# A fused attention and mixer kernel: the opening dealt anew, the x of 20 units transposed by DMA, and the last group split into two PSUM banks

## The chip, the cores and the metric

The kernel runs on one core of a Trainium2 chip. The metric is the device time of one execution in microseconds. Before the change, the median of three runs is 374.11 us (373.75 to 374.95).

## What is computed

```python
def _attn_ref(q, k, v):                       # (8, 12, 448, 64) each
    scores = scale * q @ k.transpose(0, 1, 3, 2) - np.log(S)
    return sigmoid(scores) @ v                # no row sum: every score stands alone

x = attn.transpose(0, 2, 1, 3).reshape(8, 448, 768)
h = np.maximum(x^T @ w_tok1, 0) @ w_tok2      # mixes the 448 tokens, 256 wide
u = x + h^T
h2 = np.maximum(u @ w_ch1, 0) @ w_ch2         # mixes the 768 channels, 1536 wide
out = u + h2                                  # (8, 448, 768), float32
```

Inputs are float32. The kernel converts them to fp16 while they are loaded, and accumulates in float32.

## The kernel before

**Units and cycles.** The 12 heads of a batch are dealt into three *units* of four heads (`NU = 3`), and the kernel goes through 24 units in 24 *cycles* c = 3b + u. For one unit, `qk` (L137) makes the scores, in seven steps j of 64 keys: four 64x64 matmuls into one two-bank PSUM tile (tag "qk", two of them), then one ACT sigmoid of 128x896 into `att`. `av` (L162) multiplies `att` with v into two PSUM banks and DVE casts them to `xT`, x with channels on the partitions. x is then turned so that tokens are on the partitions (`xn`), in one of two ways: `xtrans` (L197) with eight PE transposes and a DVE copy, or `xtrans_dma` (L191) with one DMA transpose issued by SP. `tok1` (L213) and `ytrans` (L240) are the token mixer; `ytrans` ends with a DVE addition into `ut`, which is u with channels on the partitions.

**The channel mixer** of a batch, `stage2` (L434), needs `ut` of all three units. `ch1` makes 12 blocks of 6 matmuls (448 columns each), `ch2` six groups of 12 matmuls (384 columns), `ch2_last` (L338) the last 64 tokens in 24 matmuls that use half the array each; DVE adds u and SP issues the output's DMAs. For batches 1 to 7, u comes from `un`, a DMA transpose of `ut` (`utrans`, L262); batch 0 has no `un`, and PE adds u with further matmuls against the identity.

**How they are woven.** The loop at L537 emits, for each cycle, the scores of that cycle's unit and the rest of the work of the unit before, and cuts `stage2` of an earlier batch into small pieces that `work(share)` pours in at three places of every cycle. `starts` (L535) says in which cycle a batch's pieces begin, and the pieces are spread evenly over the shares until the next start. `ON_DMA` (L534) says which units' x is turned by DMA. For those, `tok1` and `ytrans` come one cycle later than for units turned by PE (`mixed`, L541). A batch's `utrans` comes with its last unit's `ytrans`.

**k and q.** They must be transposed before `qk`. Batches 0 and 1 do this on PE (`pe_transpose`, L123: 14 transposes and a DVE copy, tag "m"). From batch 2 on, DVE regroups them (`relayout`, six copies, L97, recorded at L103) and SP issues two DMA transposes (`dma_transpose`, recorded at L116: `tr_k`, then `tr_q`) at the end of the cycle with u = 1 of the batch before. All use one queue of SP, which issues in program order and also carries `xtrans_dma`, `utrans` and the outputs.

**Loads.** All inputs are loaded by POOL's queue, in program order (from L381), with at most eight of them outstanding. After the opening's loads, a copy to `gate` (L602) holds back the loads of the next batches until `tr_q` of the batch in between has landed.

**The opening.** Units 0 to 2 are woven by hand (the table `between`, L476), then the *fourth cycle* (L513 to L532): the scores of unit 0 of batch 1 woven with the chain av, xtrans, tok1, ytrans of batch 0's unit 2, and the first two blocks of ch1. `keep_warm` (L449) issues matmuls on a constant while PE would wait for the first loads. PSUM tiles other than the scores' share four banks (tag "m").

Of the kernel before, what the change touches and what calls it, by code (L numbers as in the profile page):

```python
# [10 lines left out]
FP32 = mybir.dt.float32  # L11
# [9 lines left out]
NJ = 7  # L21
# [5 lines left out]
def kernel(  # L27
# [59 lines left out]
    def load(b, t, src, u0, u1):  # L87

        for g in range(2):
            dst = raw_tile(b, t)[64 * g : 64 * g + 64, u0:u1, :, :, :]  # L90
            heads = src[b, 6 * g + 2 * u0 : 6 * g + 2 * u1]
            nc.gpsimd.dma_start(  # L92
                out=dst.rearrange("p u hi j e -> p (u hi) (j e)"),
                in_=heads.rearrange("h (p j) e -> p h (j e)", j=NJ),
            )
# [27 lines left out]
    def pe_transpose(b, t, u, j0=0, j1=NJ):  # L123
        if j0 == 0:
            tps[t] = pp.tile([128, NJ, 128], FP16, tag="m", bufs=4, name=f"tp_{t}_{b}_{u}")
        ps = tps[t]
        for j in range(j0, j1):
            for hi in range(2):
                nc.tensor.transpose(  # L129
                    out=ps[64 * hi : 64 * hi + 64, j, :],  # L130
                    in_=raw[b, t][:, u, hi, j, :],
                    identity=ident[:, :],
                )
        nc.vector.tensor_copy(out=tr_tile(b, t)[:, u, j0:j1, :], in_=ps[:, j0:j1, :])
# [62 lines left out]
    def xtrans(b, u):  # L197
        ps = pp.tile([128, 4, 2, 128], FP16, tag="m", bufs=4, name=f"xb_{b}_{u}")
        for g in range(2):
            for t in range(4):  # L200
                nc.tensor.transpose(  # L201
                    out=ps[:, t, g, :],
                    in_=xTs[b % 2][:, u, g, 128 * t : 128 * t + 128],
                    identity=ident[:, :],
                )
        nc.vector.tensor_copy(
            out=xn_tile(b)[:, u, :, :, :].rearrange("s g t d -> s t g d"),
            in_=ps[:, :, :, :],
        )
# [27 lines left out]
            else:  # L237
                nc.scalar.activation(out=dst, in_=src, func=RELU)  # L238

    def ytrans(b, u, in_qk_slot=False):  # L240
        if in_qk_slot:
            both = pp.tile([128, 2, 512], FP32, tag="qk", bufs=2, name=f"yt_{b}_{u}")
        for g in range(2):
            db = NU * g + u
            if in_qk_slot:
                ps = both[:, g, :]
            else:
                ps = pp.tile([128, 512], FP32, tag="m", bufs=4, name=f"yt_{b}_{db}")
            for tcb in range(2):
                nc.tensor.matmul(  # L250
                    out=ps[:, 0:S],
                    lhsT=h1[b][:, tcb, g, u, :],
                    rhs=w2[:, tcb, :, :],
                    start=(tcb == 0),
                    stop=(tcb == 1),
                )
            nc.vector.tensor_tensor(  # L257
                out=uts[b % 2][:, db, 0:S], in0=xTs[b % 2][:, u, g, 0:S], in1=ps[:, 0:S], op=ADD
            )
# [76 lines left out]
                )  # L336

    def ch2_last(b, n0=0, n1=NCB):  # L338
        if n0 == 0:
            acc[b] = pp.tile([128, 512], FP32, tag="m", bufs=4, name=f"c2_{b}_3")  # L340
        ps = acc[b]
        for n in range(n0, n1):
            for g in range(2):
                nc.tensor.matmul(  # L344
                    out=ps[64 * g : 64 * g + 64, 0:DH],
                    lhsT=h2[b][:, n, 384:448],
                    rhs=c2[:, n, DH * g : DH * g + DH],
                    start=(n == 0),
                    stop=(n == NCB - 1 and b in un),
                )  # L350
        if n1 < NCB:
            return
        o = pa.tile([128, DH], FP32, tag="outl", bufs=2, name=f"o_{b}_3")
        if b in un:
            for g in range(2):
                part = slice(64 * g, 64 * g + 64)
                nc.vector.tensor_tensor(
                    out=o[part, :].rearrange("s (u d) -> s u d", d=128),
                    in0=un[b][0:64, NU * g : NU * g + NU, 3, :],
                    in1=ps[part, 0:DH].rearrange("s (u d) -> s u d", d=128),  # L360
                    op=ADD,
                )
        else:
            for n in range(NU):
                for g in range(2):
                    nc.tensor.matmul(
                        out=ps[64 * g : 64 * g + 64, 128 * n : 128 * n + 128],
                        lhsT=uts[b % 2][:, NU * g + n, 384:448],
                        rhs=ident[:, :],
                        start=False,  # L370
                        stop=(n == NU - 1),
                    )
            nc.vector.tensor_copy(out=o[:, :], in_=ps[:, 0:DH])
        for g in range(2):
            nc.sync.dma_start(
                out=orow[b, NJ - 1][:, DH * g : DH * g + DH],
                in_=o[64 * g : 64 * g + 64, :],
            )


# [8 lines left out]
    nc.vector.memset(w1[64:128, 3, :], 0.0)  # L389
    load(0, "q", q, 1, 2)  # L390
    load(0, "k", k, 1, 2)
    load(0, "v", v, 0, 1)
    tok_rows = moe_w_tok1.rearrange("(p j) t -> j p t", j=NJ)
    for par in range(2):
# [3 lines left out]
            in_=tok_rows[0:6].rearrange("(t par) p c -> par p t c", par=2)[par],  # L398
        )
    nc.gpsimd.dma_start(out=w1[0:64, 3, :], in_=tok_rows[NJ - 1])  # L400
    load(0, "q", q, 2, NU)
    load(0, "k", k, 2, NU)
    nc.gpsimd.dma_start(
        out=w2s[:, :, :], in_=moe_w_tok2.rearrange("(tc t) s -> t tc s", tc=2)
    )
# [4 lines left out]
    def load_c1(half):  # L410
        cols = slice(CC // 2 * half, CC // 2 * half + CC // 2)
        nc.gpsimd.dma_start(
            out=c1[:, :, cols],
            in_=moe_w_ch1.rearrange("(db d) c -> d db c", db=NDB)[:, :, cols],
        )
# [2 lines left out]
    load(1, "q", q, 1, 2)  # L418
    load(1, "k", k, 1, 2)
    load(1, "v", v, 0, 1)  # L420
    load_c1(1)
    load(1, "q", q, 2, NU)
    load(1, "k", k, 2, NU)
    load(1, "v", v, 1, NU)
    load(2, "k", k, 0, NU)
    load(2, "q", q, 0, NU)
    for half in range(2):
        part = slice(NCB // 2 * half, NCB // 2 * half + NCB // 2)
        nc.gpsimd.dma_start(
            out=c2[:, part, :],  # L430
            in_=moe_w_ch2.rearrange("(cb c) d -> c cb d", cb=NCB)[:, part, :],
        )
# [11 lines left out]

    N_CYCLES = NU * B
    N_FIRST = 4
    heat = pp.tile([128, 512], FP32, tag="m", bufs=4, name="heat")

    def keep_warm(n):  # L449
        for _ in range(n):  # L450
            nc.tensor.matmul(
                out=heat[:, 0:256], lhsT=warm[:, 0:128], rhs=warm[:, :], start=True, stop=True
            )

    keep_warm(19)
    pe_transpose(0, "q", 0)
    keep_warm(3)
    pe_transpose(0, "k", 0, 0, 2)
    pe_transpose(0, "k", 0, 2, NJ)

    def regroup_w2():
# [4 lines left out]
    def tp(b, u, t, j0=0, j1=NJ):  # L466
        return lambda: pe_transpose(b, t, u, j0, j1)
# [4 lines left out]
    def tok(u, *tcbs):  # L472
        return lambda: tok1(0, u, True, tcbs)
# [2 lines left out]
    between = [  # L476
        [
            [],
            [],
            [tp(0, 1, "q", 0, 4)],  # L480
            [tp(0, 1, "q", 4, NJ)],
            [tp(0, 1, "k", 0, 4)],
            [tp(0, 1, "k", 4, NJ)],
            [],
        ],
        [
            [value(0, 0, 3)],
            [value(0, 3, NJ)],
            [tp(0, 2, "q")],
            [lambda: xtrans(0, 0)],  # L490
            [tp(0, 2, "k"), regroup_w2],
            [tok(0, 0)],
            [tok(0, 1)],
        ],
        [
            [value(1, 0, 3)],
            [lambda: ytrans(0, 0)],
            [value(1, 3, NJ)],
            [tp(1, 0, "q")],
            [lambda: xtrans(0, 1)],  # L500
            [tp(1, 0, "k")],
            [tok(1, 0, 1)],
        ],
    ]
    for u, steps in enumerate(between):
# [4 lines left out]

    qk(1, 0, 0)  # L513
    av(0, 2, 0, 5)
    ytrans(0, 1)
    qk(1, 0, 1)
    av(0, 2, 5, NJ)
    pe_transpose(1, "q", 1)
    qk(1, 0, 2)
    xtrans(0, 2)  # L520
    ch1(0, 0, 0, 4)
    qk(1, 0, 3)
    tok1(0, 2, relu_on_vector=True)
    pe_transpose(1, "k", 1)
    ch1(0, 1, 0, 4)
    qk(1, 0, 4)
    ytrans(0, 2, in_qk_slot=True)
    qk(1, 0, 5)
    for d in (4, 5):
        for cb in range(2):  # L530
            ch1(0, cb, d, d + 1)
    qk(1, 0, 6)  # L532

    ON_DMA = range(2 * NU, N_CYCLES - 2)  # L534
    starts = [N_FIRST, N_FIRST + NU] + [NU * b + 5 for b in range(2, B - 1)] + [N_CYCLES + 1]  # L535
    pending, copies = [], []
    for c in range(N_FIRST, N_CYCLES + 1):  # L537
        b, u = divmod(c, NU)
        here = c < N_CYCLES
        before = divmod(c - 1, NU)  # L540
        mixed = [n for n in (c - 2, c - 1) if (n == c - 1) != (n in ON_DMA)]  # L541
        if c in starts:
            n = starts.index(c)
            first, slots = c, 3 * max(starts[n + 1] - c, NU)
# [35 lines left out]
        if here:  # L580
            qk(b, u, 3)
            qk(b, u, 4)
        work(2)
        for n in mixed:
            tok1(*divmod(n, NU))
        if here:
            qk(b, u, 5)
            qk(b, u, 6)
        if c == N_FIRST:
            copies = pieces  # L590
        work(3)
        for n in mixed:
            ytrans(*divmod(n, NU))
# [49 lines left out]
```

## Time and profile before

| | |
|---|---|
| median of the runs | 374.11 us |
| the profiled execution | 374.46 us, its span 372.7 us |
| mean granted TensorE clock | 0.995 |
| PE busy | 359.8 us |
| ch1 (L282), 576 matmuls | 115.8 us busy |
| ch2 (L305), 576 matmuls | 100.3 us busy |
| ACT, 168 sigmoids of 128x896 (L152) | 158.7 us busy |
| SP's queue q1 / POOL's queue q0 | 28.98 MB / 21.70 MB |
| last PE instruction ends / span ends | 368.2 us / 372.7 us |

The page gives the busy time of each engine and the groups of instructions that make it up; PE's busy time includes the latency of matmuls that overlap, so durations of a step are read below from the starts of consecutive steps. The timeline gives single steps with the idle time before them and what ended it; the stage view gives busy times, granted clock, DMA share and throughput for a stretch; the DMA view gives what each queue moved in a stretch and how long an issue took to land.

### The profile page before, as it was taken

What the parts mean: (1) busy time and instruction counts of PE and PEld (TensorE: products, weight loads), DVE (VectorE), ACT (ScalarE), POOL (GpSimd) and SP (SyncE); (2) the same over time, 40 slices, a digit from 0 to 9 for tenths busy, and PEclk for the clock granted to TensorE, in tenths of its full rate; (3) what the DMA queues carried; (4) which work ended last, traced back from release to release, by engine and by line L of the source; (5) the groups of instructions that cost most, each with busy time, mean ns of one, the idle gap of its engine ahead of it and who ended that gap; (6) DMA issues with size and microseconds to landing.
All of it is one profiled execution on the core that took longest, in us unless ns stands there. A gap on an engine that the chain in (4) does not pass through costs nothing.

```text
span 372.7 us, 7520 instructions
## 1 busy us (share of the span) xinstructions
PE 359.8 (97%) x3254; PEld 196.8 (53%) x3254; DVE 184.7 (50%) x328; ACT 171.6 (46%) x211; POOL 50.4 (14%) x87
## 2 busy tenths in 40 slices
PE   6999999999999999999999999999999999999995
PEld 4554456564545554555445555555445555565562
DVE  2466566327643655375453554465453353734532
ACT  2995544546566445455455544455444555000000
POOL 8844300500030003100040001200000000000000
PEclk9899999999999999999999999999999999999999
DMA  7999999799998697994999389974960451036014
GB/s 100 168 201 206 204 210 193 142 220 219 180 167 127 114 165 130 143 209 98 192 147 185 72 169 159 179 141 103 195 101 16 98 123 28 0 81 153 2 42 106
DMA packets 99840, 51.14 MB, mean 137 GB/s; under 512 B 73504, under 2 KB 96736, under 8 KB 99808
## 3 DMA queue, kind: packets, MB, share of 16 engines
q1 hardware_dynamic: 76384, 28.98, 42.0%
q0 software_dynamic: 23424, 21.70, 38.1%
q8 instruction: 25, 0.41, 0.4%
q14 instruction: 7, 0.06, 0.0%
HBM read 43.38 MB, written 11.01 MB: 146 GB/s over the span
## 4 chain that ended last, share of the span: by engine, by line
PE 87%; DMA 7%; ACT 2%; DVE 1%; SPq 1%; issue 1%; POOL 1%; DVEq 0%; POOLq 0%
PE c L282 26%; PE c L305 26%; PE qk L145 10%; PE xa L172 9%; DMA tr_q<-rel_q 6%; PE tk L224 5%; PE c L344 4%; PE yt L250 4%; ACT att L152 2%; PE xb L201 1%; DMA raw_k<-in_k_dram 1%; PE tp_k L129 1%; SPq L116 1%; PE tp_q L129 0%; POOL raw_q L92 0%
## 5 line engine op out<-in xcount | busy, mean ns | idle before, releaser
L152 ACT ACTIVATE att<-qk,att_bias 128x896 f16<-128x896 f32 x168 | 158.7, 1008 | 103.5 <-PE qk L145 103.5
L282 PE MATMUL c<-ut,c 128*128 128x448 f16 x576 | 115.8, 353 | 0.0
L305 PE MATMUL c<-c,h 128*128 128x384 f16 x576 | 100.3, 327 | 0.0
L290 DVE TENSOR_SCALAR h<-c 128x448 f16<-128x448 f32 x96 | 59.7, 624 | 58.7 <-PE c L282 58.6
L282 PEld LDWEIGHTS <-c 128*128 128x128 f16 x576 | 53.2, 98 | 58.3 <-issue 12.8
L305 PEld LDWEIGHTS <-h 128*128 128x128 f16 x576 | 54.0, 98 | 42.9 <-issue 9.3
L145 PE MATMUL qk<-tr_q,tr_k 64*64 64x448 f16 x672 | 53.5, 365 | 4.5 <-DMA tr_q<-rel_q 2.3
L315 DVE TENSOR_TENSOR o<-un,c 128x384 f32<-128x384 f16 x42 | 23.3, 554 | 56.6 <-PE c L305 56.0
L181 DVE CAST xT<-xa 128x448 f16<-128x448 f32 x48 | 27.7, 619 | 22.2 <-PE xa L172 22.2
L238 ACT ACTIVATE h<-tk 128x256 f16<-128x256 f32 x42 | 13.8, 381 | 52.5 <-PE tk L224 52.5
L172 PE MATMUL xa<-att,raw_v 64*64 64x448 f16 x672 | 37.6, 352 | 0.0
L257 DVE TENSOR_TENSOR ut<-xT,yt 128x448 f16<-128x448 f16 x48 | 27.6, 616 | 9.9 <-PE yt L250 9.7
L145 PEld LDWEIGHTS <-tr_k 64*64 64x64 f16 x672 | 15.6, 105 | 28.4 <-issue 25.2
L172 PEld LDWEIGHTS <-raw_v 64*64 64x64 f16 x672 | 23.5, 107 | 9.2 <-issue 0.8
L224 PE MATMUL tk<-xn,w 128*128 128x256 f16 x192 | 24.9, 273 | 0.7 <-DVE h L234 0.7
L602 POOL COPY gate<-tr_q 128x2 f16<-128x2 f16 x5 | 0.9, 184 | 164.8 <-DMA tr_q<-rel_q 164.8
L250 PE MATMUL yt<-w,h 128*128 128x448 f16 x96 | 22.2, 354 | 0.7 <-DVE ut L257 0.7
L224 PEld LDWEIGHTS <-w 128*128 128x128 f16 x192 | 18.5, 98 | 6.1 <-issue 1.2
L344 PE MATMUL c<-c,h 128*64 128x384 f16 x192 | 17.1, 328 | 0.0
L92 POOL DMA_DIRECT2D raw_k<-in_k_dram x24 | 15.2, 643 | 9.7 <-DMA c<-in_moe_w_ch_dram 4.7
L92 POOL DMA_DIRECT2D raw_q<-in_q_dram x24 | 15.5, 664 | 6.0 <-DMA c<-in_moe_w_ch_dram 4.7
L250 PEld LDWEIGHTS <-h 128*128 128x128 f16 x96 | 8.6, 98 | 10.2 <-issue 2.7
(41 smaller groups left out, 116.2 us busy)
## 6 DMA issues: line engine op xcount, KB each, us to landing
out_dram<-o SPq DMA_DIRECT2D x48, 192.0 KB, 2.7
c<-in_moe_w_ch_dram POOLq DMA_DIRECT2D x4, 1152.0 KB, 14.5
raw_k<-in_k_dram POOLq DMA_DIRECT2D x12, 336.0 KB, 5.5
raw_q<-in_q_dram POOLq DMA_DIRECT2D x12, 336.0 KB, 9.0
raw_v<-in_v_dram POOLq DMA_DIRECT2D x12, 336.0 KB, 12.1
out_dram<-o SPq DMA_DIRECT2D x16, 96.0 KB, 2.1
raw_q<-in_q_dram POOLq DMA_DIRECT2D x12, 112.0 KB, 6.6
raw_k<-in_k_dram POOLq DMA_DIRECT2D x12, 112.0 KB, 5.7
```

Source lines behind the costliest of these rows:

```text
L92: nc.gpsimd.dma_start(out=dst.rearrange("p u hi j e -> p (u hi) (j e)"), in_=heads.rearrange("h (p j) e -> p h (j e)", j=NJ),)
L145: nc.tensor.matmul(out=ps[64 * g : 64 * g + 64, hi, 0:S], lhsT=tr[b, "k"][64 * hi : 64 * hi + 64, u, j, 64 * g : 64 * g + 64], rhs=tr[b, " ...
L152: nc.scalar.activation(out=att[b, u][:, :, j, :], in_=ps[:, :, 0:S], func=SIGMOID, bias=bias_t[:, :], scale=att_scale,)
L172: nc.tensor.matmul(out=ps[g][64 * hi : 64 * hi + 64, 0:S], lhsT=raw[b, "v"][64 * g : 64 * g + 64, u, hi, j, :], rhs=att[b, u][64 * g : 64 ...
L181: nc.vector.tensor_copy(out=xTs[b % 2][:, u, g, 0:S], in_=ps[g][:, 0:S])
L224: nc.tensor.matmul(out=ps[:, tcb, :, :], lhsT=w1[:, t, cols], rhs=xn[b][:, u, :, t, :], start=(t == 0), stop=(t == 3),)
L250: nc.tensor.matmul(out=ps[:, 0:S], lhsT=h1[b][:, tcb, g, u, :], rhs=w2[:, tcb, :, :], start=(tcb == 0), stop=(tcb == 1),)
L257: nc.vector.tensor_tensor(out=uts[b % 2][:, db, 0:S], in0=xTs[b % 2][:, u, g, 0:S], in1=ps[:, 0:S], op=ADD)
L282: nc.tensor.matmul(out=ps[:, 0:S], lhsT=c1[:, BY_UNIT[d], 128 * cb : 128 * cb + 128], rhs=uts[b % 2][:, BY_UNIT[d], 0:S], start=(d == 0), ...
L290: nc.vector.tensor_scalar(out=h2[b][:, cb, :], in0=ps[:, 0:S], scalar1=0.0, scalar2=None, op0=MAX)
L305: nc.tensor.matmul(out=ps[:, 0:DH], lhsT=h2[b][:, cb, 128 * t : 128 * t + 128], rhs=c2[:, cb, cols], start=(cb == 0), stop=(cb == NCB - 1 ...
L344: nc.tensor.matmul(out=ps[64 * g : 64 * g + 64, 0:DH], lhsT=h2[b][:, n, 384:448], rhs=c2[:, n, DH * g : DH * g + DH], start=(n == 0), stop ...
```

## The change

It has five parts.

1. **Loads.** q and k of batch 0's unit 2 go ahead of v of unit 0 and the token weights. q, k of batch 1's unit 2 and k, q of batch 2 go ahead of the second half of c1 (the first weights of the channel mixer).
2. **Warm matmuls.** 21, 5 and 3 instead of 19 and 3 ahead of the first scores, and 6 + 3 new ones within unit 0's cycle.
3. **The opening's order.** q and k of unit 1 are transposed later in unit 0's cycle, in whole tiles; q of unit 2 also there; batch 0's first `ytrans` moves up into unit 1's cycle; the second stands at the head of the fourth cycle, where ch1's pieces move behind unit 2's tok1 and k's transposes ahead of it. `ytrans` of unit 2 uses the "m" banks.
4. **The loop.** `ON_DMA` grows from units 6 to 21 to units 4 to 23. Batch 0's channel work is spread over the four cycles 4 to 7 (before: 4 to 6), batch 1's over three, 8 to 10 (before: 7 to 10). Units 22 and 23 are mixed in the cycle after the last scores. In cycle 4 the relayouts are handed out a share earlier.
5. **The last group.** `ch2_last` of batch 7 adds u on PE with six matmuls against the identity, uses one bank per half, and evacuates one half on DVE and the other on ACT, whose own queue then issues that half's output.

```diff
     def ch2_last(b, n0=0, n1=NCB):
+        final = b == B - 1
         if n0 == 0:
-            acc[b] = pp.tile([128, 512], FP32, tag="m", bufs=4, name=f"c2_{b}_3")
-        ps = acc[b]
+            acc[b] = [
+                pp.tile([128, 512], FP32, tag="m", bufs=4, name=f"c2_{b}_3_{g}")
+                for g in range(2 if final else 1)
+            ]
+        parts = [slice(0, 64), slice(64, 128)]
+        ps = [acc[b][g if final else 0][parts[g], 0:DH] for g in range(2)]
+        add_on_pe = final or b not in un
...
+        for n in range(NU if add_on_pe else 0):
+            for g in range(2):
+                nc.tensor.matmul(
+                    out=ps[g][:, 128 * n : 128 * n + 128],
+                    lhsT=uts[b % 2][:, NU * g + n, 384:448],
+                    rhs=ident[:, :],
...
+        for g in range(2):
+            if final and g == 1:
+                nc.scalar.activation(out=o[parts[g], :], in_=ps[g], func=COPYF)
+            elif add_on_pe:
+                nc.vector.tensor_copy(out=o[parts[g], :], in_=ps[g])
...
+            queue = nc.scalar if final and g == 1 else nc.sync
+            queue.dma_start(
+                out=orow[b, NJ - 1][:, DH * g : DH * g + DH], in_=o[parts[g], :]
             )
...
     load(0, "q", q, 1, 2)
     load(0, "k", k, 1, 2)
+    load(0, "q", q, 2, NU)
+    load(0, "k", k, 2, NU)
     load(0, "v", v, 0, 1)
...
     load(1, "v", v, 0, 1)
-    load_c1(1)
     load(1, "q", q, 2, NU)
     load(1, "k", k, 2, NU)
-    load(1, "v", v, 1, NU)
     load(2, "k", k, 0, NU)
     load(2, "q", q, 0, NU)
+    load_c1(1)
+    load(1, "v", v, 1, NU)
...
-    keep_warm(19)
+    new_heat()
+    keep_warm(21)
     pe_transpose(0, "q", 0)
+    keep_warm(5)
+    pe_transpose(0, "k", 0, 0, 2)
     keep_warm(3)
-    pe_transpose(0, "k", 0, 0, 2)
     pe_transpose(0, "k", 0, 2, NJ)
...
     between = [
         [
             [],
-            [],
-            [tp(0, 1, "q", 0, 4)],
-            [tp(0, 1, "q", 4, NJ)],
-            [tp(0, 1, "k", 0, 4)],
-            [tp(0, 1, "k", 4, NJ)],
+            [new_heat, lambda: keep_warm(6)],
+            [lambda: keep_warm(3)],
+            [tp(0, 1, "q")],
+            [tp(0, 1, "k")],
+            [tp(0, 2, "q")],
             [],
         ],
         [
             [value(0, 0, 3)],
             [value(0, 3, NJ)],
-            [tp(0, 2, "q")],
+            [tp(0, 2, "k")],
             [lambda: xtrans(0, 0)],
-            [tp(0, 2, "k"), regroup_w2],
-            [tok(0, 0)],
+            [tok(0, 0), regroup_w2],
             [tok(0, 1)],
+            [lambda: ytrans(0, 0)],
         ],
         [
             [value(1, 0, 3)],
-            [lambda: ytrans(0, 0)],
             [value(1, 3, NJ)],
             [tp(1, 0, "q")],
             [lambda: xtrans(0, 1)],
+            [tok(1, 0)],
+            [tok(1, 1)],
             [tp(1, 0, "k")],
-            [tok(1, 0, 1)],
         ],
     ]
...
+    ytrans(0, 1)
     qk(1, 0, 0)
-    av(0, 2, 0, 5)
-    ytrans(0, 1)
+    av(0, 2, 0, 6)
     qk(1, 0, 1)
-    av(0, 2, 5, NJ)
+    av(0, 2, 6, NJ)
     pe_transpose(1, "q", 1)
     qk(1, 0, 2)
     xtrans(0, 2)
-    ch1(0, 0, 0, 4)
+    pe_transpose(1, "k", 1)
     qk(1, 0, 3)
     tok1(0, 2, relu_on_vector=True)
-    pe_transpose(1, "k", 1)
-    ch1(0, 1, 0, 4)
     qk(1, 0, 4)
-    ytrans(0, 2, in_qk_slot=True)
+    for cb in range(2):
+        ch1(0, cb, 0, 4)
+    ytrans(0, 2)
     qk(1, 0, 5)
-    for d in (4, 5):
-        for cb in range(2):
-            ch1(0, cb, d, d + 1)
+    for cb in range(2):
+        ch1(0, cb, 4, 5)
     qk(1, 0, 6)
-
-    ON_DMA = range(2 * NU, N_CYCLES - 2)
-    starts = [N_FIRST, N_FIRST + NU] + [NU * b + 5 for b in range(2, B - 1)] + [N_CYCLES + 1]
+    for cb in range(2):
+        ch1(0, cb, 5, 6)
+
+    ON_DMA = range(N_FIRST, N_CYCLES)
+    starts = [N_FIRST] + [NU * b + 5 for b in range(1, B - 1)] + [N_CYCLES + 1]
...
-        mixed = [n for n in (c - 2, c - 1) if (n == c - 1) != (n in ON_DMA)]
+        mixed = [n for n in (c - 2, c - 1) if (n == c - 1) != (n in ON_DMA) or not here]
...
+        if c == N_FIRST:
+            copies = pieces
         work(2)
...
-        if c == N_FIRST:
-            copies = pieces
         work(3)
```

More of the change, by code (lines that the diff above doesn't have):

```diff
@@ L238, in tok1, with ytrans @@
                 nc.scalar.activation(out=dst, in_=src, func=RELU)
-    def ytrans(b, u, in_qk_slot=False):
-        if in_qk_slot:
-            both = pp.tile([128, 2, 512], FP32, tag="qk", bufs=2, name=f"yt_{b}_{u}")
+    def ytrans(b, u):
         for g in range(2):
             db = NU * g + u
[L245 to L248, printed above, removed]
+            ps = pp.tile([128, 512], FP32, tag="m", bufs=4, name=f"yt_{b}_{db}")
             for tcb in range(2):
@@ L344, in ch2_last @@
                 nc.tensor.matmul(
-                    out=ps[64 * g : 64 * g + 64, 0:DH],
+                    out=ps[g],
                     lhsT=h2[b][:, n, 384:448],
@@ L348, in ch2_last @@
                     start=(n == 0),
-                    stop=(n == NCB - 1 and b in un),
+                    stop=(n == NCB - 1 and not add_on_pe),
                 )
@@ L352, in ch2_last @@
             return
-        o = pa.tile([128, DH], FP32, tag="outl", bufs=2, name=f"o_{b}_3")
-        if b in un:
-            for g in range(2):
-                part = slice(64 * g, 64 * g + 64)
+        for n in range(NU if add_on_pe else 0):
[4 more added lines that the diff above has]
+                    rhs=ident[:, :],
+                    start=False,
+                    stop=(n == NU - 1),
+                )
+        o = pa.tile([128, DH], FP32, tag="outl", bufs=2, name=f"o_{b}_3")
+        for g in range(2):
[3 more added lines that the diff above has]
+                nc.vector.tensor_copy(out=o[parts[g], :], in_=ps[g])
+            else:
                 nc.vector.tensor_tensor(
-                    out=o[part, :].rearrange("s (u d) -> s u d", d=128),
+                    out=o[parts[g], :].rearrange("s (u d) -> s u d", d=128),
                     in0=un[b][0:64, NU * g : NU * g + NU, 3, :],
-                    in1=ps[part, 0:DH].rearrange("s (u d) -> s u d", d=128),
+                    in1=ps[g].rearrange("s (u d) -> s u d", d=128),
                     op=ADD,
                 )
[L363 to L377, printed above, removed]
+            queue = nc.scalar if final and g == 1 else nc.sync
+            queue.dma_start(
+                out=orow[b, NJ - 1][:, DH * g : DH * g + DH], in_=o[parts[g], :]
             )
@@ L400 @@
     nc.gpsimd.dma_start(out=w1[0:64, 3, :], in_=tok_rows[NJ - 1])
-    load(0, "q", q, 2, NU)
-    load(0, "k", k, 2, NU)
     nc.gpsimd.dma_start(
@@ L446 @@
     N_FIRST = 4
-    heat = pp.tile([128, 512], FP32, tag="m", bufs=4, name="heat")
+    heat = {}
     def keep_warm(n):
@@ L451, in keep_warm, with new_heat @@
             nc.tensor.matmul(
-                out=heat[:, 0:256], lhsT=warm[:, 0:128], rhs=warm[:, :], start=True, stop=True
-            )
-    keep_warm(19)
+                out=heat[0][:, 0:256],
+                lhsT=warm[:, 0:128],
+                rhs=warm[:, :],
+                start=True,
+                stop=True,
+            )
+    def new_heat():
+        heat[0] = pp.tile([128, 512], FP32, tag="m", bufs=4, name="heat")
+    new_heat()
+    keep_warm(21)
     pe_transpose(0, "q", 0)
+    keep_warm(5)
+    pe_transpose(0, "k", 0, 0, 2)
     keep_warm(3)
-    pe_transpose(0, "k", 0, 0, 2)
     pe_transpose(0, "k", 0, 2, NJ)
```

## The prediction

> **What bounds the kernel now.** I read the page's totals first, then the PE's waits, then the stages, then the DMA queue behind the one wait that is left.
>
> ```profile
> PE 359.8 (97%) x3254; PEld 196.8 (53%) x3254; DVE 184.7 (50%) x328; ACT 171.6 (46%) x211; POOL 50.4 (14%) x87
> ```
>
> PE is the bound: whatever leaves its stream is gained in full, and whatever makes it wait is lost in full. The view of PE's waits holds one repeated wait on a DMA, at the first scores of a batch:
>
> ```profile
> PE qk L145 <- DMA tr_q<-rel_q: 2.3, 4, 0.7
> ```
>
> Four times, 0.7 us at most: k and q transposed by SP's DMA arrive just in time in the steady batches. Batch 2's pair (tr_k, tr_q), used first at cycle 6, is not among the four: it landed at 66.9 (issue 61.66 plus 5.2), PE came at 69.22. Cycle 6 is where I look hardest, since the change brings PE there earlier. SP's part and the DMA by stage, from the timeline and the stage view (last two columns: mean busy share, GB/s):
>
> ```profile
> 56.75 4.87 SPq L116 DMA_TRANSPOSE tr_k<-rel_k  x1
> 61.66 3.30 SPq L116 DMA_TRANSPOSE tr_q<-rel_q  x1
> ```
>
> ```profile
> 56.00:58.00 2.00, 2.00 (x33) 1.33 (x25) 2.00 (x5) 2.00 (x3) 0.00 (x0) 1.00 1.16 210
> 58.00:60.00 2.00, 2.00 (x13) 1.03 (x11) 2.00 (x5) 0.43 (x1) 0.00 (x0) 1.00 1.89 153
> 60.00:62.00 2.00, 2.00 (x23) 1.13 (x22) 1.55 (x3) 0.89 (x1) 0.00 (x0) 1.00 0.61 127
> 62.00:64.00 2.00, 2.00 (x17) 1.29 (x15) 0.49 (x1) 1.01 (x2) 0.00 (x0) 1.00 1.24 266
> ```
>
> Until 58 the engines are full (1.16) with POOL's loads, the last being c2; the transposes really run from 61 to 66.3. How the queues share shows in a later xn transpose (issued at 190.8) beside loads; first 191 to 194.5, then 195 to 200:
>
> ```profile
> q0 software_dynamic: 811, 0.70, 126.1%
> ...
> xn<-xT SPq DMA_TRANSPOSE x1, 12.0
> ```
>
> ```profile
> q0 software_dynamic: 862, 0.74, 90.6%
> q1 hardware_dynamic: 862, 0.22, 32.9%
> ```
>
> For 3.7 us SP's queue (q1) moves nothing; then it gets one packet for one of the loads, 256 B against 896 B. So 256 KB took 12.0 us; the same transpose alone took 3.1 (issue 185.65).
>
> **The opening, until 40.5 (nothing, and it is swallowed).** ACT sets it:
>
> ```profile
> 8.27 12.86 ACT L152 ACTIVATE att<-qk,att_bias 128x896 f16<-128x896 f32 x14 [5.88 <-PE qk L145]
> 21.55 6.52 ACT L152 ACTIVATE att<-qk,att_bias 128x896 f16<-128x896 f32 x7 [0.42 <-PE qk L145]
> ```
>
> 21 activations at 0.92 with one gap of 0.42. The added warm matmuls lie in waits: 2 more of 0.11 us before q lands (wait 0.47), 2 more before k (0.34), 3 beside the copy that k's second half awaits (0.38), 9 in a cycle that ACT paces; uncovered they cost 0.11 each. They aim at the clock (third last column):
>
> ```profile
> 7.80:11.20 3.40, 2.12 (x38) 1.23 (x34) 1.14 (x3) 2.93 (x4) 3.40 (x7) 1.00 1.11 150
> 11.20:14.70 3.50, 3.43 (x38) 1.67 (x41) 0.92 (x3) 3.46 (x4) 3.46 (x7) 0.51 1.18 162
> ```
>
> Half clock for 3.4 us, but inside the ACT run without a gap: curing it gains nothing. The Trainium skill, "TensorE: Matmul & The Clock Gate" (HAM oscillation), asks for a PE-idle gap over about 3.4 us before the clock falls; here it fell after a stretch with 2.12 us busy of 3.40 and no wait over 0.92, so the row decides. By the rule the warm matmuls would do nothing, by the row they may keep the clock: zero in the sum either way.
>
> q and k of unit 2 pass v of unit 0 on POOL's queue: two places of 224 KB at some 150 GB/s, 3.0 us. v landed near 11.1 to 11.7 and is read at 14.18, so it comes about when it is needed (0 to 1 us late).
>
> Walking units 1 and 2 by the rows (qk 0.31 with what follows, 14 transposes 0.51, xb 0.54, tok half 0.5, yt 0.86; DVE: cast 0.58, xn 0.69, tr copy 0.61, relu 0.42): tok now directly follows xtrans and waits for xn, so unit 2's first activation comes 0.7 later and unit 3's near 30.1 instead of 28.3, with one ytrans (0.86) more done. In the fourth cycle these waits go or shrink:
>
> ```profile
> 37.28 0.54 PE L250 MATMUL yt<-w,h 128*128 128x448 f16 x2 [0.71 <-DVE ut L257]
> 40.50 0.38 PE L145 MATMUL qk<-tr_q,tr_k 64*64 64x448 f16 x4 [0.87 <-ACT att L152]
> ```
>
> New ones come: xtrans for the cast (0.6), tok for xn (0.5). By the walk cycle 4's av starts near 40.5, before 40.68: 0.2 gained, between 1.5 gained and 1 lost.
>
> **Cycles 4 and 5.** Batch 0's work is spread over 12 shares, not 9: per share 12 matmuls of 0.19 instead of 15. Cycle 4 took 14.86 (40.68 to 55.54); less 12 matmuls, 12.6. Cycle 5, 55.54 to 69.22: unit 4's xtrans (0.54), tok (0.97) and ytrans (0.85) leave, work falls from 8.57 to 6.6: 9.35 from av to the scores of cycle 6. PE arrives at 40.5 + 12.6 + 9.35 = **62.4**.
>
> Half of c1 now lands behind 1,792 KB more: at 205 GB/s 9 us later, near 46.5 (before 23.20 + 14.4); block 6 is multiplied near 50, so it costs nothing with 3 us to spare. Batch 2's k, q land before 41 and wait for nobody. The relayouts start a share earlier, the last of k ends 12 us after av: tr_k is issued near **52.4**, 4.3 us sooner.
>
> But all loads together are as many bytes in a full queue, so c2 still ends at 58 to 61. tr_k at 52.4 stands in front of that queue: first packet some 3.7 us later, then one 256 B packet per 1,536 B packet of c2, a few hundred of its 2,688 before c2 is out. What remains, nearly 1.3 MB, takes the 5.3 us that it took before. A little is won (tr_q no longer waits for SP's issue): I take tr_q at **66.3**. Bounds: 61.6 if nothing hindered it (52.4 plus the 9.2 from 92.01 to 101.2); 64.4 if no DMA time were lost (c2 out at 58.5, 5.3 for the pair, 0.6 until the landing shows); 68 if mixing delays c2's last packets. The Trainium skill, "DMA: Bandwidth & Descriptors" (Queues, rings and completion order), says that an engine round-robins between queues per packet; the alternation agrees, the 3.7 us of nothing does not. By the rule alone tr_k would get some 400 packets more before c2 ends: 0.4 us less in the sum.
>
> So the wait moves from cycle 4 to cycle 6, 3.9 us, and a faster or slower opening only changes its length.
>
> **From cycle 6 on,** measured from its scores (69.22 before), PE does more: 24 matmuls of batch 0's second layer at 0.163 = 3.91, two additions 0.32, unit 4's tok and ytrans 1.82: +6.05. It does less: xtrans of units 5, 22 and 23, start to next start 0.54 + 0.54 + 0.45 = 1.53, as in
>
> ```profile
> 60.13 0.61 PE L201 MATMUL xb<-ident,xT 128*128 128x128 f16 x8
> ```
>
> xn by DMA there: unit 5's beside loads, up to 12.8 us after about 70, needed at 85; unit 23's with 7 us of work ahead of it: hidden. If they weren't, tok waits for the rest. Cycle 8 now has the steady shape (un ahead of tr_k on SP), so cycle 9 may get the steady wait of 0.6: +0.5.
>
> **The tail.**
>
> ```profile
> 368.21 1.13 DVE L357 TENSOR_TENSOR o<-un,c 64x384 f32<-64x384 f16 x2 [1.52 <-PE c L344]
> 368.78 1.11 SPq L375 DMA_DIRECT2D out_dram<-o  x2
> ```
>
> Six more matmuls cost 0.26 (82.88 to 83.14 in batch 0's last group); the second DVE half (0.57) goes beside the first, on ACT: between the relu's 0.38 for 256 columns and the sigmoid's 1.01 for 896, estimated 0.51. Its DMA goes from ACT, which no row shows; SP's issues took 0.47 to 0.64. Gain 0.3, between 0.6 and -0.6. Batch 0's last group has two copies instead of one, beside PE: nothing.
>
> **Sum.** (66.3 - 69.22) + 6.05 - 1.53 + 0.5 - 0.3 = **+1.8 us**. On the profiled execution, 374.46 (span 372.7, the 1.76 around it taken as unchanged), that is 376.3; the median of the runs, 374.11, lies 0.35 lower, so I predict **375.9 us**.
>
> **Rivals.**
> - *Not slower, but faster: the transposes come in time.* If SP's queue gets through beside c2, tr_q lands at 61.6 to 62.4 and PE does not wait: (62.4 - 69.22) + 4.7 = -2.1, 372.0 us. For it: the issue is 4.3 us earlier, out DMAs did get through beside loads. Against: the 12.0 us row. It decides from a landing before 63.4. Chance 0.14.
> - *Shared without loss:* tr_q at 64.4: -0.1, 374.0 us. For it: the engines are full either way; against: 58 to 62 moved only 127 to 153 GB/s while both ran. 0.28.
> - *Forecast,* 375.9 us: 0.44.
> - *Worse mixing:* c2 itself reaches PE late (its second half is read near 62), tr_q at 68: +3.5, 377.6 us. 0.14.
>
> Range 372.6 to 377.6: it leaves out some of the first and last. Faster by over 0.3% (about what a measurement can tell from no change) 0.14, within 0.28, slower 0.58.
>
> **What would show it.** Right: PE's waits list qk <- DMA tr_q once with 3 to 5 us, ending near 66; tr_k issued near 52 with a landing over 9 us; cycle 4's av at 39.5 to 41; no PE xb for units 4, 5, 22, 23; clock 1.00 from 11.2 to 14.7. Wrong: no such wait, or c2 ending before 57; or an opening that loses several us (v late at 14, ACT gaps), since past 66 it counts in full.

## The result and the profile after

The changed kernel takes 379.58 us (median of 5 runs, 379.25 to 380.56), the kernel before 374.01 us on the same chip (5 runs, 373.75 to 374.95). The ratio is 1.0153, with a 95% interval of 1.0131 to 1.0175: slower by 5.6 us, where +1.8 was forecast. The profiled span grew from 372.7 to 378.7 us, the mean granted clock fell from 0.995 to 0.991.

The page's totals of the changed kernel:

```profile
PE 361.4 (95%) x3244; PEld 197.8 (52%) x3244; DVE 181.9 (48%) x322; ACT 172.3 (45%) x212; POOL 50.9 (13%) x87
```

PE executes 10 matmuls fewer than before and is busy 1.6 us longer, and its share fell from 97% to 95%. So part of the loss is matmuls that run slower, part is waiting. PE's waits (us in total, times, longest):

```profile
PE qk L145 <- DMA tr_q<-rel_q: 7.2, 6, 4.0
PE c L300 <- DMA c<-in_moe_w_ch_dram: 1.5, 1, 1.5
```

Before, tr_q was waited for 2.3 us in all and c2 not at all. The wait of 4.0 us is the one forecast for cycle 6; the other five are the steady ones, 0.6 us each on average. SP's part of the timeline shows what brings it:

```profile
52.09 10.43 SPq L116 DMA_TRANSPOSE tr_k<-rel_k  x1
62.56 3.74 SPq L116 DMA_TRANSPOSE tr_q<-rel_q  x1
```

SP reaches tr_k 4.66 us earlier than before (56.75), but its issue instruction holds SP for 10.43 us instead of 4.87. SP can therefore issue tr_q only at 62.56, later than before (61.66). tr_k landed 13.0 us after its issue, tr_q 5.1. The DMA view gives what the queues moved from 56 to 60 (packets, MB, share of 16 engines; q0 is POOL's queue, q1 SP's):

```profile
q0 software_dynamic: 450, 0.68, 93.7%
q1 hardware_dynamic: 479, 0.12, 22.5%
```

One packet for one, 256 B of tr_k against 1.5 KB of c2, as forecast. In the 3.6 us after the issue (52 to 55.7) q1 does not appear at all; its first packet moves at 56.0. PE's timeline then shows both waits and what follows them:

```profile
63.17 0.65 PE L300 MATMUL c<-c,h 128*128 128x384 f16 x3 [1.49 <-DMA c<-in_moe_w_ch_dram]
67.82 0.96 PE L145 MATMUL qk<-tr_q,tr_k 64*64 64x448 f16 x8 [4.00 <-DMA tr_q<-rel_q]
68.54 2.86 PE L172 MATMUL xa<-att,raw_v 64*64 64x448 f16 x28
```

The last line matters most: the same 28 matmuls of av take 1.52 us in cycle 4 (start 39.88) and 1.49 in cycle 7 (82.46). The stage view explains it (length; busy time of PE, PEld, DVE, ACT, POOL; then granted clock, DMA share, GB/s):

```profile
64.00:66.00 2.00, 0.00 (x0) 0.00 (x0) 0.00 (x0) 0.00 (x0) 0.00 (x0) 0.93 1.28 269
66.00:70.00 4.00, 2.18 (x24) 1.28 (x28) 0.00 (x0) 1.48 (x2) 1.96 (x4) 0.50 0.76 134
70.00:72.50 2.50, 2.50 (x23) 1.08 (x16) 1.07 (x2) 1.10 (x2) 2.50 (x5) 0.50 1.10 167
```

PE stands still from 64 to 66; by the trace's records the clock is at half from 65.72, 1.9 us into the wait, to 72.55. In the opening it is the other way round:

```profile
11.20:14.70 3.50, 2.98 (x65) 1.95 (x65) 1.87 (x3) 3.50 (x5) 3.50 (x6) 1.00 1.23 181
```

The half clock that the kernel before shows there (0.51) is gone. The tail is as described:

```profile
374.37 0.33 PE L356 MATMUL c<-ident,ut 128*64 128x128 f16 x6
374.74 0.55 DVE L368 COPY o<-c 64x384 f32<-64x384 f32 x1 [1.68 <-PE c L356]
374.77 0.48 ACT L366 ACTIVATE o<-c 64x384 f32<-64x384 f32 x1 [40.49 <-PE c L356]
375.29 0.55 ACTq L377 DMA_DIRECT2D out_dram<-o  x1
```

DVE and ACT evacuate side by side. From PE's last instruction (374.7) to the end of the span it is 4.0 us now, 4.5 before.

**Theory** at this point: the loss is one place, cycle 6, with two parts. tr_k, issued into the load queue, delays c2 and holds SP, so tr_q lands 1.5 us later than forecast; and the wait of 4.0 us drops PE's clock for what follows. **Rivals:** the loss is spread (unit 4 and 5's work moved past cycle 6, more steady waits); or it comes from the new load order or the opening.

### The profile page after: what moved, and what is told of

Read it like the earlier page. It is cut to its first block, busy times and chain, and to the rows that moved or that the text cites. A ratio compares the mean times of both kernels' runs of the same rounds, so it can differ in the third digit from the quotient of the medians.

```text
span 378.7 us, 7505 instructions
## 1 busy us (share of the span) xinstructions
PE 361.4 (95%) x3244; PEld 197.8 (52%) x3244; DVE 181.9 (48%) x322; ACT 172.3 (45%) x212; POOL 50.9 (13%) x87
## 4 chain that ended last, share of the span: by engine, by line
PE 83%; DMA 10%; ACT 2%; DVE 2%; SPq 2%; issue 1%; POOL 0%; POOLq 0%
PE c L300 25%; PE c L277 25%; PE qk L145 10%; PE xa L172 9%; DMA tr_q<-rel_q 9%; PE tk L224 5%; PE c L345 4%; PE yt L245 4%; ACT att L152 2%; SPq L116 2%; DMA raw_k<-in_k_dram 1%; DVE xT L181 1%; PE tp_k L129 1%; DVE xn L206 0%; POOL raw_q L92 0%
## 5 line engine op out<-in xcount | busy, mean ns | idle before, releaser
L300 PEld LDWEIGHTS <-h 128*128 128x128 f16 x576 | 54.2, 98 | 44.9 <-issue 11.0
L172 PE MATMUL xa<-att,raw_v 64*64 64x448 f16 x672 | 38.5, 359 | 0.0
L172 PEld LDWEIGHTS <-raw_v 64*64 64x64 f16 x672 | 24.4, 109 | 9.1 <-issue 1.7
L366 ACT ACTIVATE o<-c 64x384 f32<-64x384 f32 x1 | 0.5, 485 | 40.5 <-PE c L356 40.5
```

The costliest lines, as they stand in the source:

```text
L172: nc.tensor.matmul(out=ps[g][64 * hi : 64 * hi + 64, 0:S], lhsT=raw[b, "v"][64 * g : 64 * g + 64, u, hi, j, :], rhs=att[b, u][64 * g : 64 ...
L300: nc.tensor.matmul(out=ps[:, 0:DH], lhsT=h2[b][:, cb, 128 * t : 128 * t + 128], rhs=c2[:, cb, cols], start=(cb == 0), stop=(cb == NCB - 1 ...
```

## The experiments

Every ratio is against the kernel before on the same chip, with its 95% interval.

**1. Matmuls on a constant ahead of the wait.**

```diff
+        if c == 2 * NU:
+            new_heat()
+            keep_warm(36)
```

> The changed kernel with 36 warm matmuls (3.9 us at full clock) ahead of cycle 6's first scores, where PE waited 4.0 us for tr_q. Theory (the wait is set by the DMA, and the half clock from 65.7 to 72.6 behind it is a second cost of its own): the data still lands near 67.8, the clock stays at 1.00, and the 4.7 us of PE work that ran at half clock take 2.4 us less: about 377.2 us. Rival (the half clock costs nothing, since something else holds PE there): 379.6 us as the changed kernel. If warm matmuls themselves delay the scores: 380 us or more.

Measured: 376.39 us, 1.005 [1.003, 1.007]. PE's timeline of this kernel at cycle 6:

```profile
64.01 4.09 PE L452 MATMUL heat<-warm 128*128 128x256 f16 x36
68.11 0.57 PE L145 MATMUL qk<-tr_q,tr_k 64*64 64x448 f16 x8
68.48 1.52 PE L172 MATMUL xa<-att,raw_v 64*64 64x448 f16 x28
```

The transposes are no earlier (tr_k 52.04 and 10.71 long, tr_q 62.79), PE goes on no earlier, but the clock stays at 1.00 and av takes 1.52 instead of 2.86. From the first scores to cycle 7's av it is 12.38 us (68.11 to 80.49), in the changed kernel 14.64 (67.82 to 82.46): 2.3 us that only the clock costs. The profiled spans differ by more, 3.1 us (375.6 against 378.7): the five steady waits are shorter too, 2.1 us in all instead of 3.2, for no reason that I could find. The medians differ by 3.2 us, the ratios by some 3.9, since the kernel before was 0.5 us slower on this chip.

**2. The second half of c2 is not loaded.** Blocks 6 to 11 multiply the first half's rows instead: as many matmuls on other numbers, so that only the time is read.

```diff
-    for half in range(2):
+    for half in range(1):
...
-                rhs=c2[:, cb, cols],
+                rhs=c2[:, cb % 6, cols],
...
-                    rhs=c2[:, n, DH * g : DH * g + DH],
+                    rhs=c2[:, n % 6, DH * g : DH * g + DH],
```

> The changed kernel without the load of c2's second half (1,152 KB); blocks 6 to 11 of the second layer multiply the first half's rows instead, so this part of the computation is changed and only the time is read. Theory (tr_k and tr_q are held up by the loads queued ahead of them): loads end near 57 instead of 62.8, SP's issue of tr_k falls from 10.4 to 4 to 6 us, tr_q lands near 61 to 63, the wait at cycle 6 is at most 1 us, the wait for c2 is gone, the clock does not fall: 372 to 373 us. Rival (the transposes are slow by themselves, or the loop's new shape costs the time elsewhere): 378 to 379.6 us.

Measured: 372.37 us, 0.9935 [0.9912, 0.9958]. SP's timeline, and below it PE's, of this kernel:

```profile
52.04 4.80 SPq L116 DMA_TRANSPOSE tr_k<-rel_k  x1
56.88 3.32 SPq L116 DMA_TRANSPOSE tr_q<-rel_q  x1
```

```profile
62.33 0.57 PE L145 MATMUL qk<-tr_q,tr_k 64*64 64x448 f16 x8 [0.20 <-DMA tr_q<-rel_q]
62.70 1.52 PE L172 MATMUL xa<-att,raw_v 64*64 64x448 f16 x28
```

The issue is at the same time, but takes 4.80 instead of 10.43, and tr_q lands when PE arrives. The whole loss is gone: it is c2 that stands between the early issue and an early landing. This run also tests the rest of the forecast's sum, as a whole and not term by term: with PE at 62.33 its terms give (62.33 - 69.22) + 4.72 = -2.2 us, and the profiled spans differ by -1.9 (370.8 against 372.7).

**3. Units 4 and 5 back on PE, batch 0 spread as before;** the rest of the change stays.

```diff
-    ON_DMA = range(N_FIRST, N_CYCLES)
-    starts = [N_FIRST] + [NU * b + 5 for b in range(1, B - 1)] + [N_CYCLES + 1]
+    ON_DMA = range(2 * NU, N_CYCLES)
+    starts = [N_FIRST, N_FIRST + NU] + [NU * b + 5 for b in range(2, B - 1)] + [N_CYCLES + 1]
```

> The changed kernel with units 4 and 5 turned by PE again and batch 0's work spread over three cycles as before; opening, loads, units 22 and 23, and the last group stay as changed. Theory (only the earlier arrival at cycle 6 costs): PE comes to cycle 6 near 68.4, about when tr_q lands, no clock fall; the gains of the rest remain, 0.8 (opening) + 1.0 (two xtrans) + 0.2 (last group): about 372 us. Rival (the opening, the load order or the last group costs): 375 us or more.

Measured: 374.17 us, 0.9979 [0.9959, 0.9999]. The loss is gone, since PE now has work until about 70, but less is gained than expected. tr_k, issued even earlier (50.49), still takes 10.79 us of SP, c2 is still waited for (1.4 us), and av of cycle 6 starts at 70.23, later than before (69.62), although cycle 4's av (39.77) was 0.9 earlier. The opening's gain is handed back at c2.

**4. The loop's part alone,** put on the kernel before.

```diff
-    ON_DMA = range(2 * NU, N_CYCLES - 2)
-    starts = [N_FIRST, N_FIRST + NU] + [NU * b + 5 for b in range(2, B - 1)] + [N_CYCLES + 1]
+    ON_DMA = range(N_FIRST, N_CYCLES)
+    starts = [N_FIRST] + [NU * b + 5 for b in range(1, B - 1)] + [N_CYCLES + 1]
...
-        mixed = [n for n in (c - 2, c - 1) if (n == c - 1) != (n in ON_DMA)]
+        mixed = [n for n in (c - 2, c - 1) if (n == c - 1) != (n in ON_DMA) or not here]
...
+        if c == N_FIRST:
+            copies = pieces
         work(2)
...
-        if c == N_FIRST:
-            copies = pieces
         work(3)
```

> The kernel before with the loop's change alone (units 4 to 23 by DMA, batch 0 over four cycles, relayouts a share earlier); its opening, load order and last group as before. Theory: the loop alone makes the loss: PE comes to cycle 6 some 0.8 us later than in the changed kernel and waits 3 to 4.5 us, the clock falls: 379.5 to 380.5 us. Rival (the new load order or opening is needed for the loss): 372 to 375 us.

Measured: 376.72 us (374.97 to 378.68), 1.006 [1.0035, 1.0085]. SP's and PE's timeline of this kernel:

```profile
52.86 8.16 SPq L116 DMA_TRANSPOSE tr_k<-rel_k  x1
```

```profile
66.52 0.96 PE L145 MATMUL qk<-tr_q,tr_k 64*64 64x448 f16 x8 [3.57 <-DMA tr_q<-rel_q]
67.23 2.70 PE L172 MATMUL xa<-att,raw_v 64*64 64x448 f16 x28
```

The loop alone makes the wait and the half clock (66.24 to 69.65), so they don't come from the opening. But the loss is smaller than expected: in this profile c2 is not waited for (its second half landed at 61.0, in the changed kernel at 63.1), tr_k's issue takes 8.16 us, and the half clock lasts 3.41 us, not 6.83. The length differs between executions: this one has a mean clock of 0.994, the twelve have 0.986 to 0.995. So the change's other parts, meant for other places, seem to make cycle 6 worse.

**5. Experiment 3, and tr_k, tr_q ahead of un on SP's queue.**

```diff
-            if n % NU == 2 and n > NU:
-                utrans(n // NU)
...
+        for n in mixed:
+            if n % NU == 2 and n > NU:
+                utrans(n // NU)
```

(the second place is behind the two `dma_transpose` calls)

> Units 4 and 5 back on PE and batch 0 over three cycles (as in the third experiment, 0.2% under the kernel before), and SP issues tr_k and tr_q ahead of un instead of behind it. In that experiment's profile PE waits four times for tr_q in the steady batches, 2.5 us in all. Theory (SP's queue order makes these waits: un's issue of 3.6 us stands ahead of tr_k): they go, un still lands before the second layer needs it, 2 us less, about 0.7% under the kernel before. Rival (the relayouts on DVE set the time of tr_k, or un now comes late): no change or slower than the third experiment.

Measured: 371.79 us, 0.9915 [0.9894, 0.9936]. Every wait for tr_q is gone from PE's waits (in experiment 3: 2.5 us in all), and 2.4 us by the two ratios are gained. So the steady wait comes from un standing ahead of tr_k on SP: turning that order round removes it. The wait for c2 (1.7 us) is still there.

**6. Experiment 3 with the old load order.**

```diff
+    load_c1(1)
     load(1, "q", q, 2, NU)
     load(1, "k", k, 2, NU)
+    load(1, "v", v, 1, NU)
     load(2, "k", k, 0, NU)
     load(2, "q", q, 0, NU)
-    load_c1(1)
-    load(1, "v", v, 1, NU)
```

> The third experiment (units 4 and 5 back on PE) with the old load order from batch 1's unit 2 on: half of c1 and v ahead of batch 2's k, q. In the third experiment tr_k was issued at 50.5, ran in front of c2's queue, and PE waited 1.4 us for c2. Theory (an early tr_k takes turns from c2 and brings c2 late): with k, q later tr_k is issued some 2 to 3 us later, c2 is in time, the wait of 1.4 us goes: 1 to 1.4 us less than the third experiment. Rival (the wait for c2 comes from the load order's own bytes, not from tr_k): the wait stays or grows, no gain.

Measured: 372.73 us, 0.994 [0.9921, 0.9959]. It is a little faster than experiment 3, but not for the stated reason: tr_k was issued at 50.25, not later, and the wait for c2 stayed (2.0 us). (The profiled execution is the slowest of the twelve, 375.67 us, the others 371.9 to 373.5; the size of that wait need not be theirs.) That part of my theory fell: the load order does not set when tr_k is issued. Why it helps stays open.

**7. The changed kernel with six transposes per batch,** one for each unit's k and q.

```diff
-    def dma_transpose(b, t):
+    def dma_transpose(b, t, u):
-            out=tr_tile(b, t).rearrange("e u j r -> e (u j) r"),
-            in_=rel[b, t].rearrange("r u j hi e -> r (u j hi e)"),
+            out=tr_tile(b, t)[:, u, :, :],
+            in_=rel[b, t][:, u, :, :, :].rearrange("r j hi e -> r (j hi e)"),
...
-                lambda t=t, n=n: relayout(b + 1, t, n) for t in ("k", "q") for n in range(NU)
+                lambda t=t, n=n: relayout(b + 1, t, n) for n in range(NU) for t in ("k", "q")
...
-            for t in ("k", "q"):
-                dma_transpose(b + 1, t)
+            for n in range(NU):
+                for t in ("k", "q"):
+                    dma_transpose(b + 1, t, n)
```

> The changed kernel with tr_k and tr_q of every batch from 2 on split by unit: six DMA transposes in the order k, q of unit 0, then 1, then 2, and the relayouts in that order. Cycle 6's first scores then wait for a third of the bytes. Theory (the wait at cycle 6 is the time that 1,376 KB of transposes need beside and behind c2): unit 0's pair lands near 63.5, the wait for tr_q falls from 4.0 to at most 1 us, the clock does not fall, the wait for c2 (1.5) stays, the steady waits of 0.6 go: 379.6 - 3 - 2.4 - 3 = about 371 us. Rival (nothing of SP's queue moves until c2 is out, or six issues cost more than two): wait 3 us or more and the clock falls, 377 to 380 us.

Measured: 374.47 us, 0.9985 [0.9962, 1.0008]: the loss of the changed kernel is gone, the expected gain is not there. PE's timeline of this kernel shows most of the reason:

```profile
64.26 0.57 PE L145 MATMUL qk<-tr_q,tr_k 64*64 64x448 f16 x8 [0.23 <-DMA tr_q<-rel_q]
...
78.30 1.51 PE L172 MATMUL xa<-att,raw_v 64*64 64x448 f16 x26 [1.30 <-DMA raw_v<-in_v_dram]
```

Cycle 6 hardly waits for tr_q any more (0.23), but cycle 7's av waits for v of batch 2. Its load is held by the copy to `gate`, which needs the last piece of tr_q, at 69.8. A PE that comes faster through cycle 6 meets the next transfer. One cycle on, av waits another 0.9 us for DVE, and the wait for c2 (1.5) is unchanged. The four slowest of the twelve executions (374.95 to 377.37 us) have mean clocks of 0.990 to 0.994, the profiled one 0.999: in some of them the clock still falls.

**8. Experiment 6 with the six transposes.** The diff is that of 7, put on 6.

> The split by unit on the kernel with units 4 and 5 back on PE and the old load order. Theory: no wait for tr_q or c2 at cycle 6 and no steady waits: 0.9 to 1.2% under the kernel before, 370 to 371 us; units 4 and 5 by DMA (the other kernel with the split) should be worth up to 1.1 us more, unless its wait for c2 eats it. Rival (split issues delay un or xn behind them on SP's queue): 372 us or more.

Measured: 371.63 us, 0.9905 [0.9883, 0.9928], the gain expected. The waits for tr_q and v are gone; the one for c2 is not. SP's timeline, and PE's:

```profile
48.53 1.32 SPq L116 DMA_TRANSPOSE tr_k<-rel_k  x1
```

```profile
63.23 1.14 PE L300 MATMUL c<-c,h 128*128 128x384 f16 x6 [1.51 <-DMA c<-in_moe_w_ch_dram]
```

The first piece of tr_k is issued ahead of the end of c2 and lands 14.6 us later, at 63.1; c2 lands at 63.2.

**9. Experiment 8 with the relayouts a share later, as before the change.**

```diff
-        if c == N_FIRST:
-            copies = pieces
         work(2)
...
+        if c == N_FIRST:
+            copies = pieces
         work(3)
```

> The split by unit with units 4 and 5 on PE and the old loads, and the relayouts of batch 2 handed out a share later, as in the kernel before. There tr_k's first piece was issued at 48.5, took turns from c2's queue, and PE waited 1.5 us for c2's second half (its last bytes at 62.8 instead of 60.9 in the kernel before). Theory (an early transpose brings c2 late and nobody needs it early there): first issue 2 to 4 us later, c2's wait at most 0.5 us, PE still finds unit 0's pair in time: 1 to 1.5 us less, 1.2 to 1.4% under the kernel before. Rival (c2 is late for its own bytes): the wait stays, no gain over the split alone (0.95% under).

Measured: **370.18 us** (370.05 to 370.35), 0.9864 [0.984, 0.9887]. It beats both kernels. SP's and PE's timeline of this kernel (with units 4 and 5 on PE, c2 is first used in cycle 5; cycle 6's scores start at 68.65):

```profile
53.54 1.34 SPq L116 DMA_TRANSPOSE tr_k<-rel_k  x1
```

```profile
60.10 0.57 PE L145 MATMUL qk<-tr_q,tr_k 64*64 64x448 f16 x8
60.61 2.12 PE L300 MATMUL c<-c,h 128*128 128x384 f16 x12
62.57 0.33 PE L318 MATMUL c<-ident,ut 128*128 128x128 f16 x3
```

The 12 matmuls with c2 run through without a wait, and there is none for tr_q. The one edit between 8 and 9 issues the first transpose 5.0 us *later*, and it lands 7.5 us after that, at 61.1: 2 us *earlier* than in 8. c2 lands at 60.4 instead of 63.2. Issued early, the transposes took turns from c2 and both were late; that is the wait of 1.5 us.

**10. The warm matmuls alone,** on the kernel before.

```diff
-    keep_warm(19)
+    new_heat()
+    keep_warm(21)
     pe_transpose(0, "q", 0)
-    keep_warm(3)
+    keep_warm(5)
     pe_transpose(0, "k", 0, 0, 2)
+    keep_warm(3)
...
-            [],
-            [tp(0, 1, "q", 0, 4)],
+            [new_heat, lambda: keep_warm(6)],
+            [lambda: keep_warm(3), tp(0, 1, "q", 0, 4)],
```

> The kernel before with the change's warm matmuls alone (21, 5 and 3 ahead of the first scores, 6 and 3 in unit 0's cycle). In the prediction these were worth nothing, since the half clock lies under an ACT run without a gap: by that, no change (0.2% either way). Rival, from the timed executions of the kernel before: their mean clock ranges from 0.985 to 1.00 and the slower ones have the lower clock, so the half clock may last longer than the 3.4 us of the profiled one: clock 1.00 in all executions and 0.2 to 0.4% less.

Measured: 374.01 us (373.51 to 374.83), 0.9968 [0.9953, 0.9983]. All its executions have a mean clock of 0.997 to 1.00. Those of the kernel before on that chip have 0.984 to 1.00, and on the whole the lower the clock, the longer they are: 374.17 us at 0.998, 376.75 at 0.984. The forecast's "curing the half clock gains nothing" fits the one profiled execution, whose half clock lay under ACT's run, and failed over the others: 0.3%, 1.2 us. Experiments 1 to 3 and 5 to 9 have these matmuls too, so a part of this size of their ratios has nothing to do with cycle 6.

## Why the prediction was too low

The wait was the forecast one, at the forecast place, but two of the steps behind the number failed. Point by point:

- **Opening.** Cycle 4's av at 39.88, forecast 40.5 within 39.2 to 41.7. v of unit 0 and the second half of c1 are not among PE's waits, but c1 was close: it landed at 49.0, forecast 46.5, and was needed at 49.5, so 0.5 us were to spare and not 3. Right otherwise, but for the warm matmuls (experiment 10).
- **PE at cycle 6.** It arrived at 63.8, of which 1.49 is the wait for c2: 62.3 without it, forecast 62.4. That close a match is partly luck: the opening was 0.6 us better than forecast, cycle 4 as forecast (12.6), and cycle 5 took 9.9 us without the wait instead of 9.35. tr_k's issue: 52.09, forecast 52.4. Right.
- **The transposes: the first step that failed.** I put tr_q at 66.3, arguing that "tr_q no longer waits for SP's issue". It did: tr_k's issue instruction stretched to 10.43 us and kept SP until 62.5. Behind that lies c2's end, which I had taken as unmoved: its last bytes came at 62.8 (before: 60.9). That tr_k's turns make c2 late is shown by experiments 8 and 9. But a part of the delay here is older: at 56, before tr_k's first packet, POOL's queue had moved 9.89 MB against 10.09 before, about 1 us at the 205 GB/s of its loads (an estimate); where that comes from stays open. PE resumed at 67.82, **+1.5 us**; the bound for worse mixing (68) held it. That the wait for tr_q came out as forecast (4.00, forecast 3.9) is chance, since the wait for c2 moved its start by 1.5 us as well.
- **The clock: the second, and the larger.** The forecast counts a wait of 3.9 us and stops at its end. The trace shows the clock at half until 72.55: 67.82 to 72.55 is 4.73 us at half speed, 2.4 us of lost work, and experiment 1 measured 2.3. No term of the sum, and no rival, held it. The Trainium skill, "TensorE: Matmul & The Clock Gate" (HAM oscillation), gives a PE-idle gap over about 3.4 us as what drops the clock. The trace has such a gap (4.00) and half clock with it, although the clock fell 1.9 us into the gap already. I had weighed that rule for the opening's short gaps but not for the long gap that I was forecasting myself.
- **From cycle 6 on.** One more steady wait, as forecast, and each 0.6; in all 0.9 us more than before instead of 0.5. The rest of the terms is borne out, as a sum, by experiment 2. The tail gained about 0.4 (forecast 0.3): from the last group's first matmul to the end of the span it is 6.3 us (372.39 to 378.7), before 6.7 (366.03 to 372.7), with ACT's copy at 0.48 (estimate 0.51).

The account: (67.82 - 69.22) + 4.72 = 3.3, plus 2.3 for the clock, plus 0.4 for the steady waits, is 6.0; the spans differ by 6.0. The rivals for the loss fell: without the c2 load, with all else in place, nothing is lost (experiment 2). The load order and the opening seem to have a share only in that they worsen cycle 6 (4 against the changed kernel); how that share divides between them was not tried.

"In time" (372.0) failed for the reason given against it, the 12.0 us row; it is what experiment 2 gives (372.37) with half of c2 out of the way.

## What to carry to other kernels

A transfer that is issued earlier into a queue that is already full gains little or nothing: here tr_k was issued 4.7 us earlier and landed 1.3 us later (65.1 instead of 63.7), in experiment 4 3.9 us earlier and landed 0.5 earlier (63.2). It takes turns from what is in front, and that can come late as well. Ask what the queue still holds at the moment of issue, and issue small pieces in the order of their use once little is left in it. And when you forecast that an engine will wait, follow the clock past the end of the wait: here 4.0 us of waiting on PE cost another 2.3 us after it.

## What the runs showed of the hardware

- A transpose on SP's queue beside a deep POOL queue moves nothing for 3.8 to 3.9 us in the changed kernel and in experiments 1 and 3 to 9, and then gets one packet for one (479 to 450). Where under 0.6 MB of loads was left at the issue, the time without any was shorter: 1.3 us in the kernel before (at 56.75), 1.9 in experiment 2. The Trainium skill, "DMA: Bandwidth & Descriptors" (Queues, rings and completion order), states the turns between queues; the trace agrees on the turns, and no rule there covers the time without any.
- SP's issue instruction of the same transpose was longer the earlier it came, with more of c2 still in the load queue: 4.87 us at 56.75 (before), 8.16 at 52.86 (experiment 4), 10.43 at 52.09, 11.24 at 50.55 (experiment 5); with half of c2 left out it was 4.80 at 52.04. SP issued tr_q only when it was over.
- The half clock came in lengths of about 3.41 us: once with a wait of 3.57, beginning 3.3 us into it (experiment 4), twice on end (6.83) with one of 4.00, beginning 1.9 us into it. In experiment 6's profile a wait of only 2.04 us for c2 was followed by one (63.86 to 67.28), in experiment 1's a wait of 1.89 was not. So the length of a single wait does not decide alone; what does, these runs leave open.
